# Five sets of fifteen small loads into an unread buffer, issued by SyncE between the cache loads of a decode attention kernel

## The chip, the cores and the metric

The kernel runs on one core of a Trainium2 chip. The metric is the device time of one execution in microseconds (us); the time before is 1303.39 us, the median of three runs that lie between 1303.38 and 1303.41.

## The reference

One decode step of an attention block with a gate beside it, in float32. Batch 2, one query position, width D = 512, 32 query heads of 128 that share 8 key and value heads, and a cache of 32768 positions.

```python
def reference(A_x, A_k_cache, A_v_cache, A_wq, A_wo, B_x, B_w1, B_b1, B_w2, B_b2):
    ...
    xn = _layernorm(x, axis=-1)
    s = _A_ref(xn, A_k_cache, A_v_cache, A_wq, A_wo)
    g = _silu(_B_ref(xn, B_w1, B_b1, B_w2, B_b2))
    return x + s * g
```

`_A_ref` projects the normalised row with `wq`, takes softmax(q k^T / sqrt(128)) v over the whole cache, and projects the heads with `wo`. `_B_ref` is a two-layer MLP with a squared ReLU (512 to 1792 to 512). `B_x` isn't used. The two caches hold 2 x 8 x 32768 x 128 float32 values each, 256 MiB for keys and 256 MiB for values, and each value is loaded once.

## The kernel before, in words

The work is a stream of 66 large loads through two SBUF buffers, `slots[0]` and `slots[1]` (each 128 partitions x 16384 float32, 8 MiB). Load 1 is `wq`, load 2 holds both MLP weights (`wm`, 7 MiB). Then, for each of the NS = 16 pairs of a key head and a batch row, come four loads: two halves of the keys (`kt`) and two halves of the values (`vt`). Odd loads go to slot 0 and even ones to slot 1.

SyncE (SP in the profile) issues them all. `load` (line 163; its DMA is line 169) waits until TensorE has finished with the slot's last content, then issues one DMA that adds 16 to the slot's semaphore. `release` (line 177) is called where the program has written TensorE's last use of a slot: it notes TensorE's token as the condition for that slot and writes the next load into SP's program behind it. So two loads are under way or in use at any time, and load n + 2 is issued when TensorE is done with load n.

TensorE waits on the slot's semaphore for each load. For keys, `scores` (line 280) runs 64 matmuls from the slot; for values 64 more accumulate into `o_ps`. The softmax in between is short and uses VectorE and ScalarE. The three compute engines run the 16 rounds as a loop; SP's program is written out straight, without a loop.

Behind the 66th load, `release` issues the seven pieces of the output projection `wo` (4 MiB down to 128 KiB, lines 184 and 187), each with a semaphore of its own. After the last round TensorE multiplies the collected heads with the pieces as they land, VectorE forms the result from that, the gate and `x`, and SP stores it (line 443), clears the semaphores and waits for the store.

Three small loads of the inputs are issued by ScalarE at the start (ACT in the profile): `small` with 22 rows of 512 bytes, and `xb` twice with 8 rows of 512 bytes. They are queue q10 of the profile; what SP issues is q1.

Of the kernel before, what the change touches and what calls it, by code (L numbers as in the profile page):

```python
# [124 lines left out]
def build(nc, x22, x8, kt, vt, wq, wm, wo, out):  # L125
    pe, act, dve = (Looped(nc, e, n) for e, n in ((nc.tensor, "pe"), (nc.scalar, "act"), (nc.vector, "dve")))
    pool, sp = (Engine(nc, e, n) for e, n in ((nc.gpsimd, "pool"), (nc.sync, "sp")))
# [7 lines left out]
    def sb(name, *shape):  # L135
        return nc.alloc_sbuf_tensor(name, [P, *shape], F32)
# [18 lines left out]

    slot_sem = [nc.alloc_semaphore(f"slot{i}") for i in range(NSLOT)]
    piece_sem = [nc.alloc_semaphore(f"piece{i}") for i in range(len(PIECES) + 2)]
    small_sem, xe_sem, out_sem = (nc.alloc_semaphore(n) for n in ("small", "xe", "out"))
    count = [0] * NSLOT
    free = [None] * NSLOT  # L160
    issued = [0]

    def load(src, width):
        i = issued[0] % NSLOT
        issued[0] += 1
        if free[i] is not None:
            sp.wait(free[i])
        count[i] += 16
        nc.sync.dma_start(slots[i][:, 0:width], src).then_inc(slot_sem[i], 16)  # L169
        return i, (slot_sem[i], count[i])  # L170
# [6 lines left out]
    def release(token):  # L177
        free[stream.pop(0)[0]] = token
        if todo:
            stream.append(load(*todo.pop(0)))  # L180
            if not todo:
                h = 0
                for n, sem in zip(PIECES, piece_sem):
                    nc.sync.dma_start(wo_sb[:, h * D:(h + n) * D], wo[h * P:(h + n) * P].rearrange("(p h) e -> p (h e)", h=n)).then_inc(sem, 16)
                    h += n
                for u in range(2):
                    nc.sync.dma_start(wo_sb[:, h * D + u * NG * HN:h * D + (u + 1) * NG * HN],
                                      wo[h * P + u * HN:h * P + (u + 1) * HN].rearrange("r (t e) -> (r t) e", t=2)).then_inc(piece_sem[len(PIECES) + u], 16)
# [3 lines left out]
    t = pool.done(g.memset(ident[:, :], 0.0))  # L192
# [11 lines left out]
    for u in range(2):  # L204
# [5 lines left out]
    t = dve.done("tensor_reduce", selh[:, :], ident[:, :].rearrange("p (a h) -> p h a", h=REP), axis=AX.X, op=ALU.add)  # L210
# [10 lines left out]
    t = pe.done()  # L221
    dve.wait(t)
    t = dve.done("tensor_copy", xs[:, :], ms[:, 0:22])
    pe.wait(t, t_one)
    mm(ms[:, 32:40], mean[:, :], xs[:, 0:8], start=True, stop=True)
    t = pe.done()
    dve.wait(t)
    t = dve.done("tensor_reduce", st[:, 2:4], ms[:, 32:40].rearrange("p (d b) -> p b d", b=B), axis=AX.X, op=ALU.add)
    dve.wait(t)
    t = dve.done("tensor_tensor", xc[:, :].rearrange("p (d b) -> p d b", b=B), xs[:, 0:8].rearrange("p (d b) -> p d b", b=B),  # L230
                                 st[:, None, 2:4].to_broadcast([P, ND, B]), op=ALU.add)
    dve.wait(t)
    t = dve.done("tensor_mul", sq[:, :], xc[:, :], xc[:, :])
    pe.wait(t)
    mm(ms[:, 64:72], mean[:, :], sq[:, :], start=True, stop=True)
    t = pe.done()
    dve.wait(t)
    t = dve.done("tensor_reduce", st[:, 4:6], ms[:, 64:72].rearrange("p (d b) -> p b d", b=B), axis=AX.X, op=ALU.add)
    dve.wait(t)
    t = dve.done("tensor_scalar", st[:, 6:8], st[:, 4:6], -1.0, 1e-5, op0=ALU.mult, op1=ALU.add)  # L240
    act.wait(t)
    t = act.done("activation", st[:, 8:10], st[:, 6:8], AF.Sqrt)
    dve.wait(t)
    t = dve.done("reciprocal", st[:, 10:12], st[:, 8:10])
# [5 lines left out]
    i, t = stream[0]  # L250
    pe.wait(t_x, t, t_selg)
    for d in range(ND):
        for f in range(2):
            for c in range(NG):
                lo = d * HQ * DH + (f * NG + c) * W
                mm(sc[f][32 * c:32 * c + 32, :], xT[:, d, :], slots[i][:, lo:lo + W], start=(d == 0), stop=(d == ND - 1))
    t = pe.done()
    release(t)
    act.wait(t)
    t_q = [act.done("copy", prob[:, f, :], sc[f][:, :]) for f in range(2)]  # L260
    for f in range(2):
# [3 lines left out]
        t = pe.done()  # L265
# [14 lines left out]
    def scores(u):  # L280
        i, t = stream[0]
        pe.wait(t, t_set, t_exp[u])
        for j in range(NJ):
            for c in range(NG):
                lo = (c * NJ + j) * W
                mm(sc[u][32 * c:32 * c + 32, :], qz[:, 28 - 4 * j:60 - 4 * j], slots[i][:, lo:lo + W],
                         start=(j == 0), stop=(j == NJ - 1))
        t = pe.done()
        release(t)
        dve.wait(t)  # L290
        return t, dve.done("tensor_reduce", rm[:, u:u + 1], sc[u][:, :], axis=AX.X, op=ALU.max)

    def mlp():
# [18 lines left out]
        for j in range(FJ):  # L312
            c = j % NG
            lo = FJ * D + j * D
            mm(wb[32 * c:32 * c + 32, :], hT[:, j, :], slots[i][:, lo:lo + D], start=(j < NG), stop=(j >= FJ - NG))
        t = pe.done()
        release(t)
        act.wait(t)
        t = act.done("copy", o_sb[:, :], wb[:, :])
# [16 lines left out]
    for s in range(NS):  # L336
# [4 lines left out]
        t_s, t = scores(1)  # L341
# [3 lines left out]
        t = dve.done("tensor_reduce", r1[:, :], rm[:, :], axis=AX.X, op=ALU.max)  # L345
        pe.wait(t, *([t_rs] if t_rs else []))
        tr(ms[:, :P], r1[:, :].to_broadcast([P, P]), ident[:, :])
        t = pe.done()
        dve.wait(t)
        t = dve.done("tensor_reduce", mh[:, :], ms[:, :P].rearrange("p (a h) -> p h a", h=REP), axis=AX.X, op=ALU.max)  # L350
        dve.wait(t)
        t = dve.done("tensor_mul", mm4[:, :], mh[:, :], seln[:, :])
        dve.wait(t)
        t = dve.done("tensor_reduce", nm[:, :], mm4[:, :], axis=AX.X, op=ALU.add)
# [5 lines left out]
        for u in range(2):  # L360
# [3 lines left out]
            t = pe.done()  # L364
# [4 lines left out]
        t = pe.done()  # L369
        dve.wait(t)  # L370
        t_rs = dve.done("reciprocal", rs[:, :], ms[:, :REP])
        for u in range(2):
            i, t = stream[0]
            pe.wait(t, t_pT[u], t_osb)
            for n in range(32):
                y = n % NG
                k, r = divmod(n, 8)
# [36 lines left out]
    for n, sem in zip(PIECES, piece_sem):  # L414
        pe.wait((sem, 16))
        for h in range(h, h + n):
            if h < WIDE:
                c = h % NG
                mm(wb[32 * c:32 * c + 32, :], heads(h, 0), wt[:, h, :], start=(h < NG), stop=(h >= WIDE - NG))
                if h == WIDE - 1:  # L420
                    t = pe.done()
# [15 lines left out]
    t = pe.done()  # L437
    dve.wait(t, t_gate)
    t = dve.done("tensor_mul", yb[:, :], gate[:, :], acc[:, :HN])
    dve.wait(t, (xe_sem, 32))  # L440
    t = dve.done("tensor_add", yb[:, :], yb[:, :], xb[:, :HN])
    sp.wait(t)
    nc.sync.dma_start(out, yb[:, :]).then_inc(out_sem, 16)
    used = sorted(x.num for x in [e.sem for e in (pe, act, dve, pool, sp)] + slot_sem + piece_sem + [small_sem, xe_sem])
    nc.sync.sem_clear(range(used[0], used[-1] + 1))
    nc.sync.wait_ge(out_sem, 16)
    for e in (pe, act, dve):
# [48 lines left out]
```

## Time and profile before

| | |
|---|---|
| median of three runs | 1303.39 us |
| span of the profiled execution, first to last instruction | 1301.8 us |
| PE (TensorE matmul) busy | 672.3 us, 52% |
| PEld (TensorE weight load) busy | 208.2 us, 16% |
| ACT, DVE, POOL busy | 78.9, 49.5 and 5.4 us |
| mean granted TensorE clock | 0.739 |
| DMA | 561.13 MB, 431 GB/s over the span |

The time that was measured for the runs and the span of the profiled execution differ by 1303.39 - 1301.8 = 1.6 us, which lies outside the first and the last instruction; no other time of the profiled execution is given. "Share" in the DMA rows is the time that packets took, as a share of the time of the core's 16 DMA engines. Packets that start in a short window can take longer than the window, so that their share there can exceed 100%. A packet of 4 bytes is the count on a semaphore with which a DMA engine ends its part of a load.

### The profile page before, as it was taken

To read this page: it belongs to the slowest core of one execution; us is meant where nothing else is said; L and a number is where in the kernel's file an instruction comes from. 1 tells how busy PE (TensorE), PEld (TensorE's weight loads), DVE (VectorE), ACT (ScalarE), POOL (GpSimd) and SP (SyncE) were. 2 spreads that over 40 slices of the span, in tenths; PEclk is the share of its full clock that TensorE was granted. 3 is DMA by queue.
4 is the path that set the end of the run, shared out by engine and by line. 5 is a ranking of instruction groups with operands and counts; after the bars stand their busy time and mean duration, and the time that the engine had idled before them with its cause. 6 is when DMAs were issued, how large, how long until landed. Compare 5 with 4: busy or idle time off the path is not lost.

```text
span 1301.8 us, 10286 instructions
## 1 busy us (share of the span) xinstructions
PE 672.3 (52%) x4671; PEld 208.2 (16%) x4671; DVE 49.5 (4%) x166; ACT 78.9 (6%) x138; POOL 5.4 (0%) x29
## 2 busy tenths in 40 slices
PE   3456455535546545545635544554554654554565
PEld 1111111201112111111212111111111211111122
DVE  0000000000000000000000000000000000000000
ACT  1010010100001010010101001010010101001010
POOL 0000000000000000000000000000000000000000
PEclk9776667677677778677767767767767767767778
DMA  9999999999999999999999999999999999999998
GB/s 406 433 446 423 445 423 447 419 441 429 429 441 427 443 425 445 423 447 419 439 431 427 443 427 443 425 445 421 447 421 439 431 427 443 427 443 425 445 421 362
DMA packets 10726, 561.13 MB, mean 431 GB/s; under 512 B 1339, under 2 KB 1633, under 8 KB 1889
## 3 DMA queue, kind: packets, MB, share of 16 engines
q1 hardware_dynamic: 10656, 561.03, 99.7%
q8 instruction: 5, 0.08, 0.0%
q10 hardware_dynamic: 65, 0.02, 0.0%
HBM read 561.01 MB, written 0.03 MB: 431 GB/s over the span
## 4 chain that ended last, share of the span: by engine, by line
DMA 75%; PE 24%; issue 1%; DVE 0%; ACT 0%; SPq 0%; DVEq 0%; ACTq 0%
DMA slot<-in_vt 36%; DMA slot<-in_kt 36%; PE sc L63 12%; PE o_ps L63 11%; DMA slot<-in_wm 3%; PE wb L63 1%; DVE hT L63 0%; PE ot L63 0%; DVE o_sb L63 0%; ACT o_sb L63 0%; DVE yb L63 0%; SPq L169 0%; DVE t L63 0%; DVE oT L63 0%; DVEq L101 0%
## 5 line engine op out<-in xcount | busy, mean ns | idle before, releaser
L63 PE MATMUL sc<-slot,qz 128*32 128x512 f32 x2048 | 295.3, 741 | 300.0 <-DMA slot<-in_kt 300.0
L63 PE MATMUL o_ps<-slot,pT 128*16 128x512 f32 x2048 | 294.3, 739 | 208.9 <-DMA slot<-in_vt 208.9
L63 PEld LDWEIGHTS sc<-slot,qz 128*32 128x32 f32 x2048 | 81.1, 133 | 503.4 <-issue 503.4
L63 PEld LDWEIGHTS o_ps<-slot,pT 128*16 128x16 f32 x2048 | 69.3, 113 | 420.6 <-issue 420.6
L63 ACT ACT_TABLE_LOAD x19 | 24.4, 1283 | 650.5 <-DVE nm L63 647.6
L63 PE MATMUL tp<-ident,prob 128*128 128x128 f32 x136 | 31.0, 397 | 53.3 <-ACT prob L63 53.2
L63 DVE TENSOR_REDUCE rm<-sc 128x1 f32<-128x512 f32 x32 | 22.1, 692 | 575.1 <-PE sc L63 575.1
L63 ACT COPY o_sb<-o_ps 128x512 f32<-128x512 f32 x16 | 9.4, 585 | 504.7 <-PE o_ps L63 504.7
L63 PEld LDWEIGHTS tp<-ident,prob 128*128 128x128 f32 x136 | 23.8, 204 | 57.9 <-issue 56.1
L63 DVE TENSOR_REDUCE t<-ot 128x4 f32<-128x64 f32 x16 | 3.6, 224 | 524.0 <-PE ot L63 524.0
L63 ACT ACTIVATE prob<-sc,nm 128x512 f32<-128x512 f32 x32 | 21.7, 682 | 0.2
L63 ACT COPY pT<-tp 128x512 f32<-128x512 f32 x32 | 18.7, 585 | 13.8 <-PE tp L63 13.8
L63 PE MATMUL sc<-slot,xT 128*32 128x512 f32 x64 | 8.4, 684 | 17.5 <-DMA slot<-in_wq 17.5
L63 PE MATMUL ot<-ident,o_sb 128*128 128x128 f32 x64 | 10.1, 280 | 13.7 <-ACT o_sb L63 13.7
L63 PEld LDWEIGHTS ms<-selh,l 128*128 128x128 f32 x64 | 15.6, 334 | 0.0
L63 PE MATMUL ms<-ident,r 128*128 128x128 f32 x16 | 4.7, 294 | 20.0 <-DVE r L63 20.0
L63 PE MATMUL ms<-selh,l 128*128 128x4 f32 x64 | 13.7, 319 | 0.0
L63 PEld LDWEIGHTS ot<-ident,o_sb 128*128 128x128 f32 x64 | 6.7, 141 | 27.9 <-issue 27.9
L63 PE MATMUL wb<-slot,xT 128*32 128x448 f32 x32 | 4.6, 738 | 6.6 <-DMA slot<-in_wm 6.6
L273 POOL COPY qz<-qT 128x4 f32<-128x4 f32 x16 | 3.0, 186 | 1167.3 <-PE sc L63 1137.3
L63 PEld LDWEIGHTS ms<-ident,r 128*128 128x128 f32 x16 | 2.1, 133 | 34.1 <-issue 34.1
L63 PE MATMUL wb<-wo_sb,oT 128*32 128x512 f32 x54 | 6.2, 596 | 0.7 <-DVE oT L63 0.7
(62 smaller groups left out, 55.6 us busy)
## 6 DMA issues: line engine op xcount, KB each, us to landing
slot<-in_wm SPq DMA_DIRECT2D x1, 7168.0 KB, 38.3
wo_sb<-in_wo SPq DMA_DIRECT2D x1, 4096.0 KB, 39.3
wo_sb<-in_wo SPq DMA_DIRECT2D x1, 2048.0 KB, 43.7
wo_sb<-in_wo SPq DMA_DIRECT2D x1, 1024.0 KB, 45.8
slot<-in_kt SPq DMA_DIRECT2D x32, 29.2
slot<-in_vt SPq DMA_DIRECT2D x32, 29.2
wo_sb<-in_wo SPq DMA_DIRECT2D x1, 512.0 KB, 46.6
wo_sb<-in_wo SPq DMA_DIRECT2D x1, 256.0 KB, 46.7
```

What stands on the lines that cost most here:

```text
L63: instruction = getattr(self.e, name)(*[x(i) if callable(x) else x for x in args], **kw)
L273: return pool.done(g.tensor_copy(qz[:, 28:32], qT[:, b, hkv, :]))
```

## The change

A buffer `mark` of 75 x 32 float32 in each partition and a semaphore `mark_sem` are added. When SP's program has issued load 3, 4, 6, 8 or 42, fifteen more loads follow at once: the k-th (k = 1 to 15) copies the first 16 + k values of the first k rows of `wo` to a strip of `mark` that nothing else uses, and adds 16 to `mark_sem`. That is 75 loads with 5 x 120 = 600 rows of 68 to 124 bytes. Nothing reads `mark`. Ahead of the final store SP also waits until all 75 have landed, and `mark_sem` is among the semaphores that are cleared.

```diff
+    mark, mark_sem = sb("mark", 75, 32), nc.alloc_semaphore("mark")
...
         if todo:
             stream.append(load(*todo.pop(0)))
+            if issued[0] in (at := (3, 4, 6, 8, 42)):
+                for k in range(1, 16):
+                    nc.sync.dma_start(mark[0:k, 15 * at.index(issued[0]) + k - 1, 0:16 + k], wo[0:k, 0:16 + k]).then_inc(mark_sem, 16)
             if not todo:
...
-    sp.wait(t)
+    sp.wait(t, (mark_sem, 5 * 15 * 16))
     nc.sync.dma_start(out, yb[:, :]).then_inc(out_sem, 16)
-    used = sorted(x.num for x in [e.sem for e in (pe, act, dve, pool, sp)] + slot_sem + piece_sem + [small_sem, xe_sem])
+    used = sorted(x.num for x in [e.sem for e in (pe, act, dve, pool, sp)] + slot_sem + piece_sem + [small_sem, xe_sem, mark_sem])
```

Only SP's program changes. At its head, SP issues before the change (the rows give line, kind, tile and source, partitions x values, and how often in a row):

```order
L169 DMA slot<-in_wq 128x16384
L173 ISA
L169 DMA slot<-in_wm 128x14336
L169 DMA slot<-in_kt 128x16384 x2
L169 DMA slot<-in_vt 128x16384 x2
```

After the change, SP's rows from the end of the first set to the start of the second, around load 4, are:

```order
L184 DMA mark<-in_wo 13x29
L184 DMA mark<-in_wo 14x30
L184 DMA mark<-in_wo 15x31
L170 DMA slot<-in_kt 128x16384
L184 DMA mark<-in_wo 1x17
L184 DMA mark<-in_wo 2x18
L184 DMA mark<-in_wo 3x19
```

The two key loads, which followed each other directly, now have fifteen small loads between them and fifteen behind the second. The second place is behind load 8, the fourth set. Before, SP's rows from load 5 on were the value loads 5 and 6, the key loads 7 and 8, the value loads 9 and 10, and on in that way:

```order
L169 DMA slot<-in_vt 128x16384 x2
L169 DMA slot<-in_kt 128x16384 x2
L169 DMA slot<-in_vt 128x16384 x2
L169 DMA slot<-in_kt 128x16384 x2
L169 DMA slot<-in_vt 128x16384 x2
```

And after the change, from load 7 on:

```order
L170 DMA slot<-in_kt 128x16384 x2
L184 DMA mark<-in_wo 1x17
L184 DMA mark<-in_wo 2x18
L184 DMA mark<-in_wo 3x19
L184 DMA mark<-in_wo 4x20
```

The rows of the set go on to 15x31, and load 9 comes behind them. The order of the large loads among themselves is as before, and no instruction of TensorE, VectorE, ScalarE or GpSimd moves.

## The prediction

> **What bounds the kernel now.** I read the busy shares first, then the DMA rows, then the chain, then single loads.
>
> ```profile
> PE 672.3 (52%) x4671; PEld 208.2 (16%) x4671; DVE 49.5 (4%) x166; ACT 78.9 (6%) x138; POOL 5.4 (0%) x29
> DMA  9999999999999999999999999999999999999998
> DMA packets 10726, 561.13 MB, mean 431 GB/s; under 512 B 1339, under 2 KB 1633, under 8 KB 1889
> q1 hardware_dynamic: 10656, 561.03, 99.7%
> q8 instruction: 5, 0.08, 0.0%
> q10 hardware_dynamic: 65, 0.02, 0.0%
> DMA 75%; PE 24%; issue 1%; DVE 0%; ACT 0%; SPq 0%; DVEq 0%; ACTq 0%
> ```
>
> TensorE is busy half of the span, while SP's queue q1 fills all 16 DMA engines for 99.7% of it. The last row, the chain, gives 24% to PE, which could be read as a second bound. One stage decides that. The view of stages, with the DMA share and GB/s at the end of its rows, cuts out two load times:
>
> ```profile
> 600.00:619.35 19.35, 8.65 (x64) 2.38 (x64) 0.69 (x1) 0.00 (x0) 0.00 (x0) 0.76 1.00 434
> 619.35:638.70 19.35, 11.91 (x77) 4.80 (x77) 1.64 (x6) 3.90 (x7) 0.19 (x1) 0.76 1.00 434
> ```
>
> 19.35 us is what 8 MiB take at 434 GB/s, and the DMA share is 1.00 in both stages, whatever PE does (8.65 or 11.91 us). The chain in order of time (start, us, what) says how the next load is always there in time:
>
> ```profile
> 50.06 29.79 DMA slot<-in_kt
> 79.85 0.12 issue
> 79.97 8.86 PE sc L63 x64
> 88.83 0.02 issue
> 88.84 29.71 DMA slot<-in_vt
> 118.56 0.22 issue
> 118.77 9.92 PE o_ps L63 x64
> 128.69 0.02 issue
> 128.71 28.54 DMA slot<-in_kt
> ```
>
> A load lands some 29 us after its issue, because it first stands behind the load ahead of it. Load 6 (issued at 88.84) landed at 118.56, so load 7 lands about 19.35 us later, at 137.9; load 8 was issued at 128.71, which leaves 137.9 - 128.7 = 9.2 us before the engines would run dry. PE's part of the chain is therefore the other half of the same overlap. **The bound is the work queued on the DMA engines**, and of the 16 it is the slowest one, because a load counts as landed when all 16 have finished.
>
> How even are the 16? Each ends its part with a packet under 512 B. I count those of one load in short windows of the DMA view. First load 2, from 38.7 to 39.4 us, then load 3, from 58.0 to 58.7 and from 59.8 to 60.2:
>
> ```profile
> DMA packets 32, 1.05 MB, mean 1498 GB/s; under 512 B 16, under 2 KB 16, under 8 KB 16
> ...
> DMA packets 28, 0.92 MB, mean 1311 GB/s; under 512 B 14, under 2 KB 14, under 8 KB 14
> ...
> DMA packets 4, 0.13 MB, mean 328 GB/s; under 512 B 2, under 2 KB 2, under 8 KB 2
> ```
>
> Then load 66, from 1277.2 to 1277.7 and from 1278.9 to 1279.3 (none lies between):
>
> ```profile
> DMA packets 24, 0.39 MB, mean 787 GB/s; under 512 B 12, under 2 KB 12, under 8 KB 12
> ...
> DMA packets 8, 0.13 MB, mean 328 GB/s; under 512 B 4, under 2 KB 4, under 8 KB 4
> ```
>
> At load 2 all sixteen ended within 0.7 us. At load 3 two came over a microsecond late, and by load 66 four do, behind twelve that are close together. The lateness doesn't heal, since an engine that is always busy can't catch up. What made it fits an instruction fetch (queue q8); the first, in the window 44.0 to 44.2:
>
> ```profile
> q8 instruction: 1, 0.02, 31.1%
> ```
>
> 31.1% of 16 engines x 0.2 us is 1.00 us on one engine for that packet. So an engine among the twelve has a reserve: it must lose about 1279.3 - 1277.7 = 1.6 us before it is the last. An engine among the four has none, or only the 0.4 us by which those four differ.
>
> **The change, part by part.** *Issue on SP.* 75 more DMAs. The nearest rows are ScalarE's loads of few rows, and SP's own:
>
> ```profile
> L63 ACTq DMA_DIRECT2D xb<-in_x x2: 572/610/647, 1.6 to 2.3; - x2
> L169 SPq DMA_DIRECT2D slot<-in_kt x32: 327/328/328, 31.3 to 1211.6; - x32
> ```
>
> (ns, least/median/most.) A set of 15 holds SP for 15 x 0.33 = 4.9 to 15 x 0.65 = 9.8 us. Behind the set, the next large load is queued on SP, and TensorE waits for that one. The shortest time that SP has until then is behind load 8: 128.71 to 146.9 (load 9), 18.2 us, by this row of SP's order of time:
>
> ```profile
> 146.93 20.19 SPq L169 DMA_DIRECT2D slot<-in_vt  x2
> ```
>
> SP's idle wait for TensorE hides the issue, so it costs nothing; with that cover gone there would still be the 9.2 us of queued data. A set would have to take 18.2 + 9.2 = 27.4 us, 1.8 us per small load, before an engine ran dry.
>
> *Packets on the DMA engines.* Here no cover exists: what an engine does for `mark` comes on top of its 19.35 us per load. A large load has 128 rows on 16 engines, so 16 ends. ScalarE's loads have 22, 8 and 8 rows, 38 packets of data; their queue has 65 packets, so 27 ends, and 27 = 11 + 8 + 8: a load runs on as many engines as divide its rows, up to 16. Load k of a set (k below 16) therefore puts one row and one end on each of k engines. All five sets have 600 such pairs, and one engine gets at most one pair per load, 75, at least none.
>
> The price of a pair: ScalarE's packets were moved in the middle of the stream, eight data packets of 512 bytes in the window 7.22 to 7.62 us, and their eight ends in 9.66 to 10.06:
>
> ```profile
> q10 hardware_dynamic: 8, 0.00, 3.4%
> ...
> q10 hardware_dynamic: 8, 0.00, 1.1%
> ```
>
> 3.4% of 16 x 400 ns, by 8, is 27 ns for 512 bytes; 1.1% is 8.8 ns for an end of 4 bytes. Between the two, 68 to 124 bytes lie at 8.8 + (27 - 8.8) x 92 / 508 = 12 ns, so a pair occupies 21 ns. Packets overlap a little: the DMA row for 600 to 619.35 us is
>
> ```profile
> q1 hardware_dynamic: 144, 8.39, 100.2%
> ```
>
> 0.2% of 19350 ns, by 9 packets per engine, is 4 ns each, so a pair delays its engine by some 21 - 8 = 13 ns. From below, a pair can't be under nothing as work; from above, the slowest packet of that queue comes at the start, in the window 2.0 to 2.5:
>
> ```profile
> q10 hardware_dynamic: 2, 0.00, 5.6%
> ```
>
> 5.6% of 16 x 500 is 448 ns for a data packet and its end, before the stream ran. I take 13 ns, since its rows come out of the saturated stream. The fullest engine then loses 75 x 13 ns = 1.0 us, the average one 600 / 16 x 13 ns = 0.5 us. On an engine among the twelve both stay under 1.6 us and are invisible. On one of the four late ones they move the end, by 0 to 1.0 us. The rows don't tell how many of the pairs these four get; I take the average, **+0.5 us**.
>
> [...]
>
> *The buffer and the end.* `mark` lies behind the other buffers and moves none of them. SP's new wait stands ahead of the store; the last set is issued behind load 42 of 66, at about 42 x 19.35 = 810 us or before, and must have landed a load time later, some 450 us ahead of the store. Nothing.
>
> *Below nothing.* The engines have no idle time to win (1.00, 434 GB/s). If another order of packets spared the four their lateness, 1.6 us (0.12%) is all there is.
>
> *Sum.* 1301.8 us span + 0.5 = 1302.3; the median of the runs lies 1.6 us above the span, so 1303.39 + 0.5 = **1303.9 us**. A measurement of this kernel tells some 0.2% from no change, 2.6 us.
>
> **Rivals.** *1. A pair holds its engine, and the time is slower.* Fifteen rows with fifteen ends in one ring are a pattern that no row of before shows: each end might have to wait until its row is written, with nothing else moving on that engine. The place is the engine with 75 pairs. It decides when 75 pairs cost more than its reserve of 1.6 us (21 ns each), and passes 0.2% at (1.6 + 2.6) / 75 = 56 ns, or at 35 ns if that engine is a late one. At 56 ns the time is 1306.0; at 448 ns it is 1303.4 + 33.6 - 1.6 = 1335.4. For it speaks the 448 ns packet; against it that ends in the stream cost 9 ns, and that 144 packets filled 100.2% with no hole at the 16 ends. The output store takes 1.5 us from issue to landing:
>
> ```profile
> out<-yb SPq DMA_DIRECT2D x1, 32.0 KB, 1.5
> ```
>
> With that price for each pair it would be 1303.4 + 112.5 - 1.6 = 1414. Chance 0.13 in all, most of it near the lower end.
>
> [...]
>
> *2. None of it shows:* the four late engines get hardly a pair. Then 1303.4. Chance 0.22.
>
> *3. One more instruction fetch.* SP's program grows by 75 DMAs, and a fetch costs its engine 1.0 us and the packet that it cuts into more, up to the 1.6 us seen. On a late engine that gives 1303.4 + 0.5 + 1.3 = 1305.2. [...] Chance 0.04.
>
> *4. Faster:* the lateness goes, 1303.4 - 1.6 = 1301.8; nothing in the rows names a reason. Chance 0.03: 0.01 for this, which stays within 0.2%, and 0.02 for a cause outside all this that gives more.
>
> **How the numbers follow.** The forecast, 1303.5 to 1304.6, has the remaining 0.58. Cases that stay within 0.2%: 0.58 + 0.22 + 0.04 + 0.01 = 0.85; slower 0.13; faster 0.02. The range goes from 1303.2 to 1306.0: it leaves out rival 4 and most of rival 1, some 0.15.
>
> **What would show it.** In the changed profile q1 should have 10656 + 1200 = 11856 packets and 2539 under 512 B; 19.35 us per load and share 1.00 in the stages without a set; SP's 15 issues over long before the next large load; the twelve early ends of load 66 spread wider, up to 1.0 us, and the last end at most 1.0 us later than 1279.3. More than 4 us between early and late ends would show rival 1; a sixth packet on q8 rival 3; a stage with a DMA share clearly under 1 behind a set would prove the hiding of SP's issue wrong.

## The result, and the profile after

The changed kernel takes 1312.96 us (median of three, 1312.67 to 1313.1) against 1303.39: 9.6 us more, a ratio of 1.0072 with a 95% interval of 1.0054 to 1.009. The prediction of 1303.9 with a range up to 1306.0 was wrong. The span of the profiled execution grew as much, from 1301.8 to 1311.5 us.

The DMA rows of the page of the changed kernel:

```profile
DMA packets 11927, 561.20 MB, mean 428 GB/s; under 512 B 2539, under 2 KB 2833, under 8 KB 3089
q1 hardware_dynamic: 11856, 561.09, 99.4%
q8 instruction: 5, 0.08, 0.0%
q10 hardware_dynamic: 65, 0.02, 0.0%
q14 instruction: 1, 0.01, 0.0%
```

The 1200 packets are there, 11856 and 2539 as worked out, and q8 has its five packets as before, not the sixth of rival 3. One instruction packet more is there all the same, on q14: 8 KB at 296.4 us, 0.31 us long, far from the 9.6. Still 99.4% busy, at 428 GB/s instead of 431: the engines are "busy" and move less. SP's own order of time (start, us, what), around the first set and the fourth:

```profile
32.14 0.33 SPq L170 DMA_DIRECT2D slot<-in_kt  x1
32.52 5.36 SPq L184 DMA_DIRECT2D mark<-in_wo  x15
52.64 0.36 SPq L170 DMA_DIRECT2D slot<-in_kt  x1
...
131.67 5.23 SPq L184 DMA_DIRECT2D mark<-in_wo  x15
152.22 20.38 SPq L170 DMA_DIRECT2D slot<-in_vt  x2
```

A set holds SP for 5.2 to 5.4 us and is over long before the next large load (131.67 + 5.23 = 136.9 against 152.22). The issue costs nothing, as forecast. The ends of load 66, counted as before in windows, here 1282.5 to 1283.6, 1283.6 to 1284.4, 1284.4 to 1287 and 1287 to 1289.2 us:

```profile
DMA packets 18, 0.49 MB, mean 447 GB/s; under 512 B 7, under 2 KB 7, under 8 KB 7
...
DMA packets 8, 0.26 MB, mean 328 GB/s; under 512 B 2, under 2 KB 2, under 8 KB 2
...
DMA packets 33, 0.98 MB, mean 378 GB/s; under 512 B 5, under 2 KB 5, under 8 KB 5
...
DMA packets 32, 0.98 MB, mean 447 GB/s; under 512 B 2, under 2 KB 2, under 8 KB 2
```

Twelve ends within 0.5 us and four 1.6 us behind have become sixteen ends spread over more than 5 us, the last ten us later than before. That is what the prediction named as the mark of rival 1. Where the time goes is seen in the stages (DMA share and GB/s stand last), one after the second set and one far from any:

```profile
78.00:82.00 4.00, 0.78 (x4) 0.23 (x8) 0.00 (x0) 0.00 (x0) 0.00 (x0) 0.50 1.00 347
...
600.00:619.35 19.35, 9.93 (x68) 2.98 (x68) 0.39 (x2) 0.16 (x1) 0.00 (x0) 0.74 1.00 434
```

Share 1.00 in both, but 347 GB/s against 434. A packet counts as busy for as long as it takes, and one behind this set took 4.48 us instead of 2.42 (both below), so the share hides the stall and the rate shows it. In a window as short as 4 us, though, rate and share both depend on which packets happen to start in it, and only one divided by the other can be compared. In the kernel before, the same 4 us are

```profile
78.00:82.00 4.00, 2.03 (x12) 0.68 (x16) 0.00 (x0) 0.00 (x0) 0.00 (x0) 0.50 0.68 295
```

295 GB/s at a share of 0.68 is 434 per full share, as far from any set; 347 at 1.00 is a fifth less. In the changed kernel 58 to 62 us give 417 / 1.22 = 342, and 118 to 122 us 412 / 1.15 = 358.

The times at which the counts of the large loads reach their semaphores settle the place. The last count of the first load behind each set (loads 4, 5, 7, 9 and 43) comes 1.3, 2.9, 5.2, 7.5 and 9.8 us later than before. From load 9 to load 42, with no set between, that delay grows by only 0.3 us, and a load takes its 19.35 us again (the last counts of loads 9 and 10 land at 184.10 and 203.44). Each set leaves its engines further apart: the sixteen counts of loads 4, 5, 7 and 9 land within 3.1, 4.6, 6.8 and 9.1 us.

The chain in order of time shows the same from TensorE's side, around the third and fourth sets (start, us, what):

```profile
131.28 31.47 DMA slot<-in_kt
162.75 0.12 issue
162.87 9.37 PE sc L63 x64
172.24 0.02 issue
172.25 31.19 DMA slot<-in_vt
203.44 0.22 issue
203.66 9.44 PE o_ps L63 x64
213.10 0.02 issue
213.12 29.05 DMA slot<-in_kt
```

Load 8, issued at 131.28, runs behind load 7, which the third set holds up; load 10, issued at 172.25, runs behind load 9, which the fourth holds up. They take 31.5 and 31.2 us from issue to landing instead of 28.5 to 29.8; load 12, with no set ahead of the load before it, takes 29.05. TensorE's part is about as long as before. The time is lost in the DMA engines, near the sets.

### The profile page after: what moved, and what is told of

It reads as the page before. It is cut to its first block, busy times and chain, and to the rows that moved or that the text cites. A ratio compares the mean times of both kernels' runs of the same rounds, so it can differ in the third digit from the quotient of the medians.

```text
span 1311.5 us, 10362 instructions
## 1 busy us (share of the span) xinstructions
PE 678.3 (52%) x4671; PEld 208.6 (16%) x4671; DVE 49.5 (4%) x166; ACT 79.0 (6%) x138; POOL 5.4 (0%) x29
## 2 busy tenths in 40 slices
DMA packets 11927, 561.20 MB, mean 428 GB/s; under 512 B 2539, under 2 KB 2833, under 8 KB 3089
## 3 DMA queue, kind: packets, MB, share of 16 engines
q1 hardware_dynamic: 11856, 561.09, 99.4%
## 4 chain that ended last, share of the span: by engine, by line
DMA 76%; PE 23%; issue 0%; DVE 0%; SPq 0%
DMA slot<-in_kt 36%; DMA slot<-in_vt 34%; PE sc L63 12%; PE o_ps L63 11%; DMA wo_sb<-in_wo 3%; DMA slot<-in_wm 3%; PE wb L63 1%; DVE hT L63 0%; SPq L188 0%; SPq L170 0%; DVE o_sb L63 0%; DVE yb L63 0%; SPq L174 0%
## 5 line engine op out<-in xcount | busy, mean ns | idle before, releaser
L63 PE MATMUL ms<-selh,l 128*128 128x4 f32 x64 | 13.6, 319 | 0.0
```

Source lines behind the costliest of these rows:

```text
L63: instruction = getattr(self.e, name)(*[x(i) if callable(x) else x for x in args], **kw)
```

## The experiments

My first theory (A) was that an engine reads only a few packets ahead, so that the 64 KB packet behind a burst of small ones starts late. Its first rivals were a price for each end of a load (B) and a disturbance by the 600 rows taken together (C); D to G came up as runs spoke against these, and each is stated where it is first tried.

The kernels below are the changed one with the lines shown put in place of its set of loads; `mark` and the final wait are sized to match, and `...` within a line stands for the strip that a load writes, or for a source as before. Each difference is taken between medians, the kernel before being run beside it. The first four ask whose time it is.

**One engine alone.** All rows of a set go to one engine.

```diff
-                for k in range(1, 16):
-                    nc.sync.dma_start(mark[0:k, ...], wo[0:k, 0:16 + k]).then_inc(mark_sem, 16)
+                for k in range(15):
+                    nc.sync.dma_start(mark[0:1, ...], wo[0:1, 0:31]).then_inc(mark_sem, 16)
```

> Five sets of 15 loads of one row of 124 bytes each: 75 pairs of a row and its end on one DMA engine, nothing on the other fifteen. Theory A (the engine reads a limited number of packets ahead; a burst of small ones leaves it with little data ahead, so that the 64 KB packet behind the burst waits): as the changed kernel, +9.6 us, 1313, and only that engine is late. Theory B (each end holds its engine, some 0.15 us a pair): also +9.6. Theory C (the 600 rows of all engines disturb each other or the HBM): an eighth of the rows, hidden in the 1.6 us of reserve, 1303.4 to 1304.

Measured: 1312.48 against 1303.47, +9.0, ratio 1.0069 (1.0053 to 1.0086). The 525 rows on the other engines make at most the 0.6 us between this and +9.6; theory C is out. Its windows for the ends of load 66, 1282 to 1284, 1284 to 1288.2 and 1288.2 to 1288.5:

```profile
DMA packets 39, 0.82 MB, mean 410 GB/s; under 512 B 15, under 2 KB 15, under 8 KB 15
...
DMA packets 49, 1.64 MB, mean 390 GB/s; under 512 B 0, under 2 KB 0, under 8 KB 0
...
DMA packets 11, 0.33 MB, mean 1092 GB/s; under 512 B 1, under 2 KB 1, under 8 KB 1
```

Fifteen ends together, and one engine over 4 us behind: the fullest engine sets the time. What it does in the third set is seen in two neighbouring windows, 120.43 to 120.663 and 120.663 to 120.675:

```profile
DMA packets 31, 0.00 MB, mean 8 GB/s; under 512 B 31, under 2 KB 31, under 8 KB 31
...
q1 hardware_dynamic: 1, 0.07, 2242.2%
```

One end of the large load and then fifteen pairs in 0.233 us, 15 ns a pair: the 13 ns of the forecast are there in the packets. The next packet, the first 64 KB of the next load, takes 2242.2% of 16 x 12 ns = 4.31 us. In the kernel before, the row for such a packet alone in a window (46.9 to 48.1) is

```profile
q1 hardware_dynamic: 1, 0.07, 12.6%
```

12.6% of 16 x 1.2 us, 2.42. So the price, 1.89 us a set, stands on the packet behind the burst and on no small packet.

**One load of 128 rows a set.**

```diff
+                for k in range(1):
+                    nc.sync.dma_start(mark[0:128, ...], wo[0:128, 0:31]).then_inc(mark_sem, 16)
```

> Each set is one load of 128 rows of 124 bytes: 8 rows and 1 end on each of the 16 engines, 640 rows in all. Theory A by packets: 9 small packets are like 4 to 5 pairs of the changed kernel, behind which the next packet took 2.45 to 2.54 us for 2.42; with the burst of 0.12 us that is some 0.2 us a set on every engine, +1.0, 1304.4. Theory A if only rows count: like 8 pairs, next packet 3.4 us, +5.5, 1309. Theory B: one end a set, 5 x 0.15 = +0.75. Theory C: as many rows as the changed kernel, about +10.

Measured: 1303.71 against 1303.47, ratio 1.0002 (0.9993 to 1.0012): nothing. It has 640 rows, more than the changed kernel, but only 5 ends on each engine.

**Eight loads of 16 rows a set.** The same 640 rows.

```diff
+                for k in range(8):
+                    nc.sync.dma_start(mark[0:16, ...], wo[0:16, 0:31]).then_inc(mark_sem, 16)
```

> Each set is 8 loads of 16 rows of 124 bytes: 8 rows and 8 ends on each engine, the same 640 rows as in the kernel with one load a set. Theory A: 8 pairs on every engine, next packet 3.4 us for 2.42 and a burst of 0.12: 1.1 us a set, no reserve since all engines lose alike, +5.5, 1309. If rows alone count, the same time as with one load a set. Theory B: 40 ends x 0.15 = +6. Theory C: the same as with one load a set.

Measured: 1307.83 against 1303.47, +4.4, ratio 1.0033 (1.002 to 1.0045). Equal rows, seven more ends on each engine and set, 4.1 us more: it is the ends, or the loads, that cost.

**Thirty loads a set on one engine.**

```diff
+                for k in range(30):
+                    nc.sync.dma_start(mark[0:1, ...], wo[0:1, 0:17]).then_inc(mark_sem, 16)
```

> Five sets of 30 loads of one row of 68 bytes on one engine: 150 pairs. Theory A: the stall behind a burst can't exceed the time of one read, about 2.0 to 2.3 us, and 30 pairs themselves take 0.46: 5 x 2.6 - 1.6 = +11.4, 1315. A price per pair (theory B, 0.15 us): 150 x 0.15 - 1.6 = +20.9, 1324.

Measured: 1328.63 against 1303.47, +25.2, ratio 1.0194 (1.0177 to 1.0211). Theory A falls: the stall isn't bounded by one read. In the window 126.482 to 126.49 of this kernel, the packet behind the third set of thirty:

```profile
q1 hardware_dynamic: 1, 0.07, 5338.3%
```

5338.3% of 16 x 8 ns is 6.83 us, 4.41 more than 2.42. Fifteen pairs gave 1.89, so fifteen further ones give 2.52, 0.168 us each; going back from there, as an estimate from these two, 0.63 us of the stall of a burst are hidden (15 x 0.168 - 1.89). In the changed kernel itself the packet behind one to three pairs took 2.42 to 2.47 us in its second set, behind five 2.51, behind fifteen 4.48. One to three ends held the next packet up by 0.05 us at most, which is why the 66 large loads never showed the price.

The next four ask what it depends on.

**Two sets of fifteen loads of 16 rows from SP**, and **the same thirty loads from ScalarE**, whose queue takes turns with SP's, as its rows below show.

```diff
+            if issued[0] in (at := (4, 6)):
+                for k in range(15):
+                    nc.sync.dma_start(mark[0:16, ...], wo[0:16, 0:31]).then_inc(mark_sem, 16)
```

> Two sets, behind loads 4 and 6, of 15 loads of 16 rows of 124 bytes, issued by SP: 15 pairs on every engine and set. The runs so far: the packet behind 8, 15 and 30 pairs took some 0.9, 1.9 and 4.2 us more than 2.42, so the read limit of one latency (theory A as stated) has fallen. Theory D: reading in a pair takes an engine some 0.14 us, one after the other, while the moving side needs 15 ns; a lead of some 0.35 us hides the first two or three pairs of a burst. Theory D and theory B (0.14 us for each pair wherever it stands) both give 2 x (0.23 + 1.9) = +4.2, 1307.6.

```diff
         t = act.done("activation", gate[:, :], yb[:, :], AF.Sigmoid)
+        for k in range(30):
+            act.fetch(mark_sem, mark[0:16, k, 0:31], wo[0:16, 0:31])
```

> The same 30 loads of 16 rows issued by ScalarE, ahead of its loop, on its own queue, whose packets take turns with the large ones of SP's queue. Theory D: each small packet stands alone between packets of 64 KB, so the lead is won back each time and only the 28 ns per pair of the 512 byte rows of before remain: 30 x 0.015 to 0.028 = +0.5 to +0.8, 1304. Theory B: 30 x 0.14 = +4.2, 1307.6, as from SP.

Measured: from SP 1307.66 against 1303.47, +4.2 (1.0019 to 1.0044); from ScalarE 1303.98, +0.5, ratio 1.0004 (0.9994 to 1.0014). The page of the latter has the same packets on ScalarE's queue, 65 + 960:

```profile
q10 hardware_dynamic: 1025, 0.08, 0.1%
```

Its packets take turns with the large ones; in the window 100 to 119.35 us of this run each queue has 141:

```profile
q1 hardware_dynamic: 141, 8.19, 98.2%
q10 hardware_dynamic: 141, 0.01, 0.5%
```

Taken singly between packets of 64 KB, the 30 ends on each engine cost 0.5 us in all, where the same ends from SP cost 4.2. Theory B in its form "0.14 us wherever it stands" is out.

**Rows of 1 KB**, and **rows of 4 KB**, to the unused `wo_sb`:

```diff
+                    p = 16 * at.index(issued[0])
+                    nc.sync.dma_start(wo_sb[p:p + k, 256 * k:256 * k + 251], wo[0:k, 0:251]).then_inc(mark_sem, 16)
...
+                sp.wait((mark_sem, 5 * 15 * 16))
```

> As the changed kernel, with rows of 1004 bytes instead of 68 to 124, written to the part of wo_sb that isn't loaded yet; SP waits for them ahead of the pieces of wo. Moving a pair takes some 49 ns instead of 15. Theory D: reading in still takes 0.14 us a pair and goes on beside the moving, so the time is that of the changed kernel, +9.5, 1313, and the packet behind a set waits less (some 1.5 us instead of 2.0). A price that comes on top of the moving: 75 x (0.137 + 0.049) - 1.6 = +12.3, 1315.7.

> As before with rows of 4084 bytes, which take 0.151 us each to move, 0.157 with the end. Theory D: moving now takes as long as reading in, the packet behind a set takes hardly more than 2.42 us, and the time is 75 x 0.157 - 1.6 = +10.2, 1313.6, so that rows of 40 times the bytes cost the same. A price on top: 75 x (0.137 + 0.157) - 1.6 = +20.4, 1323.8.

Measured: 1317.07 against 1303.47, +13.6 (1.0089 to 1.0122), and 1355.72, +52.3 (1.0381 to 1.0415). Both miss theory D, and the second misses everything; it is taken up below.

**Other rows for each load**, for the small size and for 4 KB, to see whether reading one place again and again is the cause:

```diff
+                    r = 53 * (15 * at.index(issued[0]) + k - 1)
+                    nc.sync.dma_start(mark[0:k, ..., 0:16 + k], wo[r:r + k, 0:16 + k]).then_inc(mark_sem, 16)
```

> The changed kernel with one thing altered: each small load reads other rows of wo (53 rows further on each time) instead of all reading the first k rows. The rows of 4 KB, all read from the same 30 rows of wo, took 0.4 to 0.6 us each where 0.16 was due, which theory D doesn't explain. Theory E: reads of one and the same place are served one after the other, some 0.14 us apart for small ones, and the small loads of a set all read the same place. By E the stalls go and the time is 75 x 0.015 us below the reserve of 1.6: 1303.4 to 1304. By D (each pair takes the engine 0.14 us to read in, wherever it reads) nothing changes: +9.5, 1313.

> The kernel with rows of 4084 bytes, each load reading other rows of wo. Theory E: the extra goes and the bytes remain, 75 x 0.157 - 1.6 = +10.2, 1313.6, with 4 KB packets of 0.16 us. If the extra belongs to the burst of packets itself, as before: 1355.7.

Measured: 1312.43 against 1303.39, +9.0 (1.0053 to 1.0086), and 1355.71, as without the edit. Theory E is out for both.

**Thirty-two rows and one end on each engine**, and **the same 75 loads, two behind each of the loads 3 to 40**:

```diff
+                h = 4 * at.index(issued[0])
+                nc.sync.dma_start(mark[:, h:h + 4, 0:31], wo[128 * h:128 * (h + 4)].rearrange("(p h) e -> p h e", h=4)[:, :, 0:31]).then_inc(mark_sem, 16)
```

> Each set is one load with 4 rows of 124 bytes in each of 128 partitions, all from different rows of wo: 32 rows and 1 end on each engine. Theory E: nothing is read twice, only the bytes and packets count, 5 x (32 x 0.010 + 0.006) = +1.6, 1305. Theory D with ends as the cost: also about +1.6. Theory D with packets as the cost (70 ns for each row and each end): 33 x 0.07 - 0.35 + 0.33 = 2.3 a set, +11.5, 1315.

```diff
-            if issued[0] in (at := (3, 4, 6, 8, 42)):
-                for k in range(1, 16):
+            if 3 <= issued[0] <= 40:
+                for j in range(2 * issued[0] - 6, min(75, 2 * issued[0] - 4)):
+                    k = 1 + j % 15
```

> The same 75 small loads as the changed kernel, two behind each of the loads 3 to 40 instead of fifteen behind each of five. Theories D and E both: one to three pairs are hidden by the lead (the packet behind them took 2.42 to 2.45 us), 75 x 0.015 us stays below the reserve of 1.6: 1303.4 to 1304. A fixed price of 0.14 us a pair: +9.5, 1313.

Measured: 1305.27 against 1303.39, +1.9 (1.0005 to 1.0024): 2560 rows cost what their bytes and packets do, a sixth of what a price per packet would make. And 1304.14, +0.75, ratio 1.0005 (0.9996 to 1.0015), not told from no change, though its page counts the same small packets as the changed kernel's:

```profile
DMA packets 11927, 561.20 MB, mean 431 GB/s; under 512 B 2539, under 2 KB 2833, under 8 KB 3089
q1 hardware_dynamic: 11856, 561.09, 99.7%
```

The same work spread out is back at 431 GB/s and 99.7%. The cost belongs to ends that follow each other closely in one queue of one engine: +9.6 us for the five sets, +0.75 for the same loads in twos.

**What an end waits for.** The trace also holds the times at which the counts reach the semaphore. I take the read away (a row from SBUF), then alter the write (a row to HBM):

```diff
+                sp.wait(t_id)
+                    nc.sync.dma_start(mark[0:1, ...], ident[0:1, 0:31]).then_inc(mark_sem, 16)
```

> Fifteen loads of one row on one engine, as in the first experiment, but the row is copied from an SBUF buffer (ident) instead of from wo in HBM. In the trace of the first experiment the counts of a set land on the semaphore some 0.185 us apart though their packets stand 15 ns apart. Theory F (each end waits until its row is written, and what is behind it on that engine waits too): the source doesn't matter, +9.0, 1312.4, counts again 0.18 us apart. Theory D (reading in a row takes 0.14 us): reading from SBUF is another price; if it is much shorter, 1303.4 to 1306.

```diff
+    mark, mark_sem = nc.dram_tensor("mark", (75, 32), F32).ap(), nc.alloc_semaphore("mark")
...
+                    nc.sync.dma_start(mark[...], wo[0:1, 0:31]).then_inc(mark_sem, 16)
```

> The same fifteen loads of one row, read from wo in HBM as in the first experiment, but written to a buffer in HBM instead of SBUF. Theory F: the wait is that for the write, so both the spacing of the counts and the time change with the target; the only row that I have for a write to HBM is the final store, 1.5 us from issue to landing, so anything up to 75 x 1.5 - 1.6 = +111; I expect counts 0.3 to 1.5 us apart and 1320 or more. Theory D: the reads are the same, so the time is that of the first experiment, +9.0, 1312.4.

Measured: 1312.19 against 1303.55, +8.6 (1.0049 to 1.0083), and 1312.71, +9.2 (1.0053 to 1.0088). Neither matters, so D (reading in the row is the price) falls with the first and F (the wait for the write of the row), as I had put it, with the second. The counts of the second set, first six of fifteen, in ns from the start of the span:

```
HBM to SBUF (first experiment)   80380  80563  80746  80929  81111  81295
SBUF to SBUF                     80305  80488  80671  80854  81037  81220
HBM to HBM                       80119  80302  80485  80667  80850  81033
HBM to SBUF, rows of 4 KB        80736  80930  81126  81310  81505  81700
```

183 ns from one to the next in the first three (up to 192 later in the set), wherever the row comes from or goes. **Each further end costs its engine as long as its count takes to follow the one before**: the counts of one engine come 0.183 us apart, although their packets are recorded 15 ns apart, and the 0.168 us by which a further pair holds up the next packet make 0.183 with these 15 ns. The semaphore doesn't set that pace: the sixteen counts of load 1 in the changed kernel, one from each engine, land within 0.34 us.

That the delivery of the count is what holds the engine is my reading, not shown. Every load here has exactly one end on each engine that it uses, so the runs don't separate the count from other work that an engine may do once for each load.

**Rows of 4 KB again**: on one engine (the last row of the table), and on fifteen with every fourth partition as target, to see whether the engines or the partitions make the price.

```diff
+                    p = (0, 1, 2, 3, 32)[at.index(issued[0])]
+                    nc.sync.dma_start(wo_sb[p:p + 1, 1024 * k:1024 * k + 1021], ...).then_inc(mark_sem, 16)
```

> Five sets of 15 loads of one row of 4084 bytes, all on one engine, into partitions 0, 1, 2, 3 and 32 of wo_sb. The counts of one engine landed 0.183 us apart for rows from HBM, from SBUF and to HBM alike. Theory G: the count itself takes the engine 0.183 us, one after the other. If a row's 0.151 us pass beside it, a pair costs what it did, about 0.18 to 0.2 less the lead: +10 to +12, 1314. If they add, 75 x (0.151 + 0.183) - 1.6 less a lead of 0.65 a set = +20, 1324. If a 4 KB row of itself costs the 0.6 us seen with fifteen engines: 75 x 0.6 - 1.6 = +43 and more.

```diff
-                    p = 16 * at.index(issued[0])
-                    nc.sync.dma_start(wo_sb[p:p + k, ...], ...).then_inc(mark_sem, 16)
+                    p = (0, 1, 2, 3, 64)[at.index(issued[0])]
+                    nc.sync.dma_start(wo_sb[p:p + 4 * k - 3:4, ...], ...).then_inc(mark_sem, 16)
```

> The kernel with rows of 4084 bytes on one to fifteen engines, each load's rows in every fourth partition instead of neighbouring ones. [...] If the partitions don't matter: 1355.7.

Measured: 1317.88 against 1303.52, +14.4, but between 1315.83 and 1321.34 from run to run, ratio 1.0119 (1.0102 to 1.0136); and 1325.03, +21.5 (1.0148 to 1.0182). On one engine the counts are 0.19 us apart and all 75 packets of 4 KB take 0.159 us. So most of the row's time passes beside its count, but not all: with counts 0.193 us apart 5 x (15 x 0.193 - 0.63) - 1.6 = +9.7 was due, with both times added some +20, and the +14.4 lies between. What the rest is stays open. With every fourth partition the packets take 0.159 to 0.355 us instead of up to 0.76, and 31 of the 52 us are gone. So most of the extra of the large rows hangs on fifteen engines writing to neighbouring partitions; the runs show this dependence on the partitions, not its reason. The +21.5 that remain, and the 4 us of the 1 KB rows, I have not taken apart.

## Why the prediction was wrong

**The bound** was right: the slowest of 16 always busy engines. The first experiment delays a single engine and the whole kernel follows (+9.0 us).

**The issue on SP** was right: 5.2 to 5.4 us a set, inside the 4.9 to 9.8 worked out, with nothing behind it late. A stage with a share under 1, which should have spoken against it, does occur, but late and for another reason:

```profile
175.00:194.35 19.35, 11.19 (x76) 4.19 (x76) 0.18 (x1) 3.72 (x7) 0.00 (x0) 0.74 0.96 417
```

417 GB/s at a share of 0.96 are 434 per full share: fewer packets start in this stage, and that alone makes no engine idle. By then the early engines are up to 9 us ahead of the last one: the sixteen counts of load 9 land between 175.0 and 184.1 us, those of load 10 between 194.4 and 203.4. Load 11 is issued at 193.2, so the earliest engine has only 1.2 us left, and four packets that start from 194.37 to 194.83 took 2.68 to 3.09 us instead of 2.42. The last engine still has 10.2 us of queued data. So early engines run short, because the sets had put them so far ahead, and the last one doesn't.

**The packets** came as counted, 600 rows and 600 ends, up to 15 pairs of a set on one engine.

**The step that failed is the price of a pair** and, with it, the loss of the fullest engine, 75 x 13 ns = 1.0 us: "I take 13 ns, since its rows come out of the saturated stream". The packet rows do show 15 ns. But the ends in those rows each stood alone behind 64 KB, where the 0.63 us that a burst hides covers one count three times over. Ends in close order, which I had called a pattern that no row of before shows, cost 0.183 us each. With that, the fullest engine loses 5 x (15 x 0.183 - 0.63) = 10.6 us instead of 1.0, and the forecast's own sum gives 10.6 - 1.6 = +9.0 us, against +9.0 for one engine alone and +9.6 for the change. The 0.63 was read from the packets of one engine alone and of thirty loads; the two runs on all engines are independent of it. For eight ends on every engine, without a reserve, 5 x (8 x 0.183 - 0.63) = +4.2 (measured 4.4); for fifteen, twice, +4.2 (4.2); for thirty on one engine 5 x (30 x 0.183 - 0.63) - 1.6 = +22.7 (25.2, of which 2.5 stay open).

**Taking the average engine** (0.5 us) was wrong too: once the fullest engine exceeds its reserve of 1.6 us, it decides (+9.0 us from that engine alone, of +9.6).

**Rival 1** had the place, the engine with 75 pairs, and the deciding point of 56 ns; the measured 9.6 + 1.6 us are 0.15 us for each of 75. I gave it 0.13. Its mechanism was half right: ends in close order do hold up what is behind them on the engine (4.31 us for 2.42 behind fifteen), but a wait for the write of the row, as I had imagined it, is not borne out, since a write to HBM in place of SBUF changed neither the time (+9.2 against +9.0) nor the spacing (183 ns). The 9 ns with which I argued against it are the length of a record; the counts follow each other in 183 ns. And I set the 448 ns aside as a packet from "before the stream ran", but that window, 2.0 to 2.5 us of the kernel before, holds packets of the stream too:

```profile
q1 hardware_dynamic: 5, 0.33, 186.4%
```

So that was no reason to set the row aside. What made its 448 ns stays open.

## What to carry to other kernels

In a kernel bound by its DMA engines, count the small loads that end on each engine in close order: an end took 0.183 us here, one to three in a row held the next packet up by 0.05 us at most, and the engine with the most set the time (+9.0 us alone, +9.6 with all fifteen). For rows of up to 124 bytes the bytes hardly counted (2560 rows: +1.9 us); with rows of 1 KB the change cost +13.6 us, with 4 KB +52.3. Spread small loads between large ones (+0.75 us here for the same 75 loads) or put them on another engine's queue (+0.5 from ScalarE, +4.2 from SP), and merge rows into one load: 2560 rows with 5 ends on each engine cost 1.9 us where 75 rows with 75 ends cost 9.0. And judge such a stage by its GB/s per share (342 to 358 here near sets, 434 elsewhere), or by GB/s over whole loads, since the packet behind a burst counts as busy for all of its 4.31 us.

## What the runs showed of the hardware beyond that

With fifteen ends on one engine alone, the packet that shows the price is the one behind the burst (4.31 us for 2.42), and not one of the small packets: 9.1% of 16 x 233 ns is 339 ns for the 31 of its third set, which at 9 ns for an end leaves 13 ns for each row. The source and the target of a small row, HBM or SBUF, changed little: 183 ns between counts in all three, and +9.0, +8.6 and +9.2 us. Fifteen engines that wrote 4 KB rows to neighbouring partitions took up to 0.76 us a packet, against 0.159 us on one engine alone.
